# Decay attention and two MLPs on one core: a later arrival for the first weights in the planner, and one copy of the row maxima per unit

## The chip, the cores and the metric

The kernel runs on one core of a Trainium2 chip. The core has five engines with instruction streams of their own: PE multiplies matrices, DVE, ACT and POOL work on vectors, and SP mainly issues transfers (DMA). An engine takes its instructions in order: one that waits holds up all behind it on its engine. The metric is the device time of one execution in microseconds (us). Three runs of the kernel before gave a median of 1074.44 us (1074.03 to 1074.98).

## The reference

Three stages, all in float32:

- attention with decay, for 4 batches of 8 heads, 576 positions, 64 wide: the scores are `q k^T / 8` plus `cum[s] - cum[t]`, where `cum` is the running sum of `log(clip(f, 1e-4, 1))`; positions behind the diagonal are masked; a softmax, with the row's maximum subtracted before the exponential; the result times `v`
- a first MLP on the 2304 rows of 512: `h = x @ w_in` (512 x 2048), `h * sigmoid(1.702 h)`, times `w_out` (2048 x 512)
- a second MLP of the same shape, with `max(h, 0) + alpha * min(h, 0)` between its two products

## The kernel before

**How float32 is multiplied.** An operand is split into a high and a low part in the format fp32r, and a product is taken as high x high, high x low and low x high. Splitting costs a rounding copy (helpers L354 on ACT, L356 on DVE) and a subtraction (L359 on DVE or POOL). Weights come through a longer conversion. `weight` calls `convert` for the half of `w_in` and the half of `w_out` that belong to 128 of the 2048 hidden columns. `convert` loads 512 KB into one of three raw buffers (`p_raw8`, L475), runs L479 and L480 on ACT, L481, L484 and L487 on DVE (the last on POOL at times), and then the split (L354, L359).

**Units of attention.** A unit is one batch, one pair of heads and one part of the positions: 0 to 255 (the first half, 16 units) or 256 to 575 (the second half, 16 units). `prep` loads and splits q, k and v. `chunk` finds the row maxima: PE computes the scores of each 128-row tile and head (L602, or L595 and L596 for a last tile of 64 rows, which holds both heads), DVE adds the mask and takes the maximum of each row into one column of a tile `MX` (L611). A matmul of `MX` with an identity turns these columns into rows of a PSUM bank (L627), and copies with the factor -1 bring the rows into `DQ` (L636 on ACT or L638 on DVE), one copy per tile and head. A turning matmul holds up to four jobs, one per tile and head, each in its own 32 columns. A unit of the first half has one such matmul and four copies, one of the second half two matmuls and six copies. A column beside each maximum holds -1.0, which gives the ones that multiply `cum` in `DK`.

`chunk2` computes the scores again, transposed, as four products per head (L663). The last of them is `DK` times `DQ` and adds the decay and subtracts the maximum; so it needs the copies. ACT takes the exponentials (L667), POOL clears what is behind the diagonal (L671), PE multiplies with v (L683, L689, L712), and DVE divides (L722 to L742) into `xr`.

**The MLPs.** As soon as 256 positions are finished for all heads, `mlp1a` runs the first 8 of the 16 weight slices over them (L755 for the hidden layer, L797 for the output), between the units of attention. After attention the other 8 slices follow (L755, L878), then the second MLP (L755, L907).

**What sets the order.** Nothing in the order is written by hand. Every operation is given to a `Plan` with its engines, its cost in ns, what it reads and writes, and a priority. `Plan.run` then goes through them when the kernel is built: it takes, again and again, the operation that can start earliest by its own account (the priority decides between equals), on the engine where it ends earliest. The engines get their instructions in that order. A transfer counts as finished at

```
end = max(t + 1500.0, dma) + dur + 750.0
```

where `dur` is its bytes over 360 and `dma` the end of the transfer before it. Whoever reads the result may start `LAT` = 230 later, plus the operation's own `lag`, which is 0 everywhere in the kernel before. The first eight weight slices are added with priorities of about 100 to 109, all others with 2000 and more. At the start POOL fills the buffers that keep constants (L417), `MX` among them (two buffers).

Of the kernel before, what the change touches and what calls it, by code (L numbers as in the profile page):

```python
# [7 lines left out]
F32 = mybir.dt.float32  # L8
# [10 lines left out]
BS = 200  # L19
WS = 0  # L20
BD = 300
QUEUE = {"SP": "SP", "ACTQ": "ACT"}


# [157 lines left out]
def kernel(  # L182
# [18 lines left out]
    P = 128  # L201
# [42 lines left out]
    def sb(reg, nm, slots, shape, dt=F32, after=()):  # L244
        p = Pool(slots, after)

        def make(i):
            side, cl = closing[reg]
            return open_region(reg, side, cl).tile(shape, dt, name=f"{nm}{i}", tag=f"{nm}{i}")

        p.make = make
        return p
# [33 lines left out]
    p_vr = sb("att", "VR", 2, [P, NKT, 2, P])  # L286
    p_vh = sb("att", "VH", 2, [P, 3, 2, P], F32R)
    p_vl = sb("att", "VL", 2, [P, 3, 3, D], F32R)
    p_mx = sb("att", "MX", 2, [P, 132], F32R)
    p_e = sb("att", "e", 4, [P, 2, 320])  # L290
    p_eh = sb("att", "eh", 2, [P, 2, 320], F32R)
    p_el = sb("att", "el", 2, [P, 2, 320], F32R)
# [68 lines left out]
    def a_copy(n):  # L361
        return [("ACT", c_act(n)), ("DVE", c_dve(n, True), BC + WC * n, True)]
# [37 lines left out]
    plan.add([("POOL", 870.0)], set_mask, (), [b_mask], -88)  # L400
    plan.add([("POOL", 700.0)], set_mask2, (), [b_mask2], -40)
    plan.add(a_copy(P), lambda e: copy(e, ident_r, ident), [b_id], [b_idr], -60)
    fill = {}
    for nm, p, view, n, val in (
        ("dk", p_dk, lambda x: (x.bitcast(F32), x[0:3].bitcast(F32), x[64:67].bitcast(F32)), 3 * S, (0.0, 1.0, 1.0)),
        ("z", p_z, lambda x: x.bitcast(F32), P, 0.0),
        ("dq", p_dq, lambda x: x.bitcast(F32), S - SPLIT, 0.0),
        ("mx", p_mx, lambda x: x.bitcast(F32), 132, -1.0),
        ("vr", p_vr, lambda x: x.rearrange("p t h c -> p t (h c)")[:, :, D:3 * D], NKT * P, 1.0),
        ("vh", p_vh, lambda x: x.rearrange("p t h c -> p t (h c)")[:, :, D:3 * D].bitcast(F32), 3 * P, 1.0),  # L410
        ("vl", p_vl, lambda x: x[:, :, 1].bitcast(F32), 3 * D, 0.0),
    ):
        for i in range(p.n):
            b = fill[nm, i] = Buf()
            p.tiles[i] = p.make(i)
            plan.add([("POOL", 0.95 * n + 60.0)], lambda e, p=p, i=i, view=view, val=val: [
                E[e].memset(x, y) for x, y in (zip(view(p.tiles[i]), val) if isinstance(val, tuple) else ((view(p.tiles[i]), val),))  # L417
            ], (), [b], -90 if nm in ("dk", "dq", "mx") and i == 0 else -70 if i == 0 else -40)
# [51 lines left out]
    def convert(wb, half, src, pri, lpri=None):  # L470

        raw, w = Buf(p_raw8), Buf(p_wc)
        sl = slice(half * KT, (half + 1) * KT)
        n = KT * P
        plan.add(DMA(P * n * 8), lambda e: nc.sync.dma_start(raw.ap.rearrange("p c n t -> p c (n t)"), src), (), [raw], pri if lpri is None else lpri)  # L475
        low, high = lambda: raw.ap[:, :, :, 0], lambda: raw.ap[:, :, :, 1]
        wi = lambda: w.ap.bitcast(I32)

        plan.add([("ACT", c_act(n))], lambda e: nc.scalar.mul(w.ap, high().bitcast(F32), 2.0 ** -112), [raw], [w], pri)  # L479
        plan.add([("ACT", c_act(n))], lambda e: nc.scalar.mul(low(), low().bitcast(U32), 2.0 ** -29), (), [(raw, 0)], pri)  # L480
        plan.add([("DVE", c_dve(n, True), 0.0, True)], lambda e: nc.vector.tensor_scalar(wi(), wi(), 3, None, op0=ALU.logical_shift_left), (), [w], pri)  # L481
        plan.add(
            [("DVE", c_dve(n), 0.0, True)],
            lambda e: nc.vector.scalar_tensor_tensor(low(), high(), -2 ** 31, low(), op0=ALU.bitwise_and, op1=ALU.bitwise_or),  # L484
            (), [raw], pri,
        )
        plan.add(a_sub(n), lambda e: E[e].tensor_tensor(wi(), wi(), low(), op=ALU.add), [raw], [w], pri)  # L487
        plan.add(a_copy(n), lambda e: copy(e, wb.ap[:, 0, sl], w.ap), [w], [(wb, (half, 0))], pri)
        plan.add(a_sub(n), lambda e: sub(e, wb.ap[:, 1, sl], w.ap, wb.ap[:, 0, sl].bitcast(F32)), [w, (wb, (half, 0))], [(wb, (half, 1))], pri)
# [82 lines left out]
    def chunk(u, q0, q1, pri):  # L572
        kh, dk, qh, dq, z = u["kh"], u["dk"], u["qh"], u["dq"], u["z"]
        mx = Buf(p_mx)
        fmx = filled("mx", p_mx)
        n = q1 - q0
        tiles = [(t, t * P, min(P, S - t * P)) for t in range(q0 // P, (q1 + P - 1) // P)]
        nt = len(tiles)

        jobs = []  # L580
        for j, (t, a, w) in enumerate(tiles):
            jobs += [(j, t, a, w, (hh,)) for hh in range(2)] if w == P else [(j, t, a, w, (0, 1))]
        ji = 0
        for j, t, a, w in [(j, *x) for j, x in enumerate(tiles)]:
            ext = a + w
            cols = []
            step = ext if ext <= 512 else ext // 2
            for c0 in range(0, ext, step):
                c1 = c0 + step
                pms = [Buf(ps_m) for _ in range(2 if w == P else 1)]  # L590

                def mm(e, pms=pms, a=a, w=w, c0=c0, c1=c1):
                    if w < P:
                        o = pms[0].ap[:, :c1 - c0]
                        nc.tensor.matmul(o, z.ap, kh.ap[:, c0:c1], start=True, stop=False)  # L595
                        nc.tensor.matmul(o, ones[:, 1], dk.ap[:, c0:c1], start=False, stop=True)  # L596
                        return
                    for x, y in ((qh, kh), (None, dk)):
                        for hh in range(2):
                            r = slice(64 * hh, 64 * hh + 64)  # L600
                            l = ones[r, 0, :w] if x is None else x.ap[r, a - q0:a - q0 + w]
                            nc.tensor.matmul(pms[hh].ap[:, :c1 - c0], l, y.ap[r, c0:c1], start=x is not None, stop=x is None)  # L602

                plan.add([("PE", 2 * c_mm(c1 - c0, P))], mm, [qh if w == P else z, kh, (dk, 0), (dk, 1), b_one, *u["fdk"]], pms, pri)
                for i, pm in enumerate(pms):
                    col = 32 * (ji + i) + (2 if c0 == 0 else 3)
                    if w == P:
                        mk, m0 = mask, 3 * P - t * P + c0
                    else:
                        mk, m0 = (mask, 0) if c1 < ext else (mask2, 0)  # L610
                    plan.add([("DVE", c_dve(c1 - c0) + 90.0)], lambda e, pm=pm, c0=c0, c1=c1, mk=mk, m0=m0, col=col: nc.vector.tensor_tensor_reduce(  # L611
                        pm.ap[:, :c1 - c0], pm.ap[:, :c1 - c0], mk[:, m0:m0 + c1 - c0], 1.0, NEG,
                        ALU.add, ALU.max, accum_out=mx.ap[:, col:col + 1],
                    ), [b_mask if mk is mask else b_mask2, *fmx], [pm, (mx, col)], pri)
                    cols.append(col)
            if w < P:
                x, y = cols
                plan.add([("DVE", 70.0, 0.0, True)], lambda e, x=x, y=y: nc.vector.tensor_tensor(
                    mx.ap[:, x:x + 1], mx.ap[:, x:x + 1].bitcast(F32), mx.ap[:, y:y + 1].bitcast(F32), op=ALU.max
                ), [(mx, y)], [(mx, x)], pri)  # L620
            ji += 2 if w == P else 1

        pt = Buf(ps_m)
        for i0 in range(0, len(jobs), 4):
            jb = jobs[i0:i0 + 4]
            rows = 32 * len(jb) - 29
            plan.add([("PE", 110.0)], lambda e, i0=i0, rows=rows: nc.tensor.matmul(  # L627
                pt.ap[0:rows, 32 * i0:32 * i0 + P], mx.ap[:, 32 * i0:32 * i0 + rows], ident_r, start=True, stop=True
            ), [mx, b_idr], [(pt, i0)], pri)
            for i, (j, t, a, w, hhs) in enumerate(jb):  # L630
                for g, hh in enumerate(hhs):
                    def ev(e, i0=i0, i=i, a=a, w=w, hh=hh, g=g):
                        d = dq.ap[64 * hh:64 * hh + 3, a - q0:a - q0 + w]
                        s_ = pt.ap[32 * i:32 * i + 3, 32 * i0 + g * w:32 * i0 + g * w + w]
                        if e == "ACT":
                            nc.scalar.mul(d, s_, -1.0)  # L636
                        else:
                            nc.vector.tensor_scalar_mul(d, s_, -1.0)  # L638

                    plan.add([("ACT", 280.0), ("DVE", 240.0)], ev, [(pt, i0), *u["fdq"]], [(dq, ("x", i0 + i, hh))], pri)  # L640
        return dict(u=u, q0=q0, q1=q1, pri=pri)

    def chunk2(x):
# [324 lines left out]
```

## Time and profile before

| | |
|---|---|
| median of 3 runs | 1074.44 us |
| the profiled execution's own time | 1074.68 us |
| its span, first to last instruction | 1072.9 us |
| granted TensorE clock, mean | 0.978 of full speed |
| PE busy | 1034.7 us (96%) |
| DVE busy | 691.2 us (64%) |
| ACT busy | 446.9 us (42%) |
| POOL busy | 125.6 us (12%) |

The page divides the span into 40 slices of 26.8 us and gives the busy share of each in tenths (9 is 90% or more). PEclk is the clock that PE was granted, in tenths of full speed.

```profile
PE   5768999999999899999999999999999999999998
DVE  5888987888888877959963359833434433444333
ACT  4557545664645565847742237411211210211111
PEclk7888999999999999999999999999999999999999
DMA  5576563332242111645653245400200100010001
```

The first four slices, some 107 us, are those in which PE is not full. Attention goes on to about 410 us, the first MLP's second part to about 690 us, and the second MLP fills the rest.

### The profile page before, as it was taken

The page shows a single profiled execution, that of the slowest core. Times are in us where ns is not written, and L with a number is a line of the kernel's source. Part 1 is how long each engine was busy: PE and PEld are TensorE (multiplying, and loading weights), DVE is VectorE, ACT ScalarE, POOL GpSimd, SP SyncE. Part 2 cuts the span into 40 slices and gives each one's busy share as a digit, 9 for nine tenths or more (in the row PEclk, how much of TensorE's full clock was granted, in tenths as well). Part 3 has the DMA queues.
Part 4 walks back from the last instruction along what each step waited for, and adds up shares of the span by engine and source line. Part 5 has one row for each costly group of instructions (what it writes and reads, how often), then busy time and mean ns, then how long its engine had stood idle before and what let it go on. Part 6 is the DMA issues. An engine that isn't in the chain of part 4 may idle for free.

```text
span 1072.9 us, 17784 instructions
## 1 busy us (share of the span) xinstructions
PE 1034.7 (96%) x6531; PEld 887.3 (83%) x6531; DVE 691.2 (64%) x1565; ACT 446.9 (42%) x1042; POOL 125.6 (12%) x192
## 2 busy tenths in 40 slices
PE   5768999999999899999999999999999999999998
PEld 3657888889998789998878898888888888898886
DVE  5888987888888877959963359833434433444333
ACT  4557545664645565847742237411211210211111
POOL 6223221120111111002100101200000000000000
PEclk7888999999999999999999999999999999999999
DMA  5576563332242111645653245400200100010001
GB/s 112 125 167 178 126 153 78 67 78 60 52 94 41 52 24 47 211 156 163 222 165 98 69 128 158 137 1 1 69 0 1 57 13 1 20 41 20 1 1 39
DMA packets 170055, 86.54 MB, mean 81 GB/s; under 512 B 127440, under 2 KB 155280, under 8 KB 169968
## 3 DMA queue, kind: packets, MB, share of 16 engines
q1 hardware_dynamic: 160720, 84.30, 28.7%
q10 hardware_dynamic: 9248, 1.12, 0.7%
q8 instruction: 51, 0.84, 0.3%
q14 instruction: 36, 0.29, 0.1%
HBM read 66.34 MB, written 19.02 MB: 80 GB/s over the span
## 4 chain that ended last, share of the span: by engine, by line
PE 89%; DMA 3%; DVE 3%; ACT 2%; POOL 1%; issue 1%; SPq 0%; ACTq 0%; POOLq 0%; DVEq 0%
PE bk L755 36%; PE bk L907 18%; PE bk L797 10%; PE bk L878 8%; PE bk L663 5%; PE bk L712 4%; PE bk L683 2%; PE bk L602 2%; DMA wraw<-in_moe_w_out_dram 1%; DMA wraw<-in_moe_w_in_dram 1%; PE bk L689 1%; DMA rk<-in_k_dram 1%; PE bk L595 1%; PE bk L627 0%; POOL DK L417 0%
## 5 line engine op out<-in xcount | busy, mean ns | idle before, releaser
L354 ACT CAST qgh<-qgg 128x512 fp32r<-128x512 f32 (+1 forms) x118 | 68.3, 579 | 334.3 <-DVE qgg L769 297.2
L766 DVE TENSOR_SCALAR qgg<-bk,alpha_sb 128x512 f32<-128x512 f32 (+1 forms) x80 | 55.4, 694 | 164.9 <-PE bk L755 164.8
L755 PE MATMUL bk<-qx,wB 128*128 128x512 f32 (+1 forms) x720 | 155.9, 368 | 0.0
L755 PEld LDWEIGHTS bk<-qx,wB 128*128 128x128 f32 x720 | 126.0, 189 | 22.6
L755 PE MATMUL bk<-xh,wA 128*128 128x256 f32 x576 | 121.5, 293 | 0.0
L359 DVE TENSOR_TENSOR qgl<-qgg,qgh 128x512 fp32r<-128x512 f32 (+1 forms) x117 | 74.7, 640 | 68.4 <-ACT qgh L354 51.8
L755 PE MATMUL bk<-qx,wA 128*128 128x512 f32 (+1 forms) x480 | 103.6, 368 | 0.0
L755 PEld LDWEIGHTS bk<-xh,wA 128*128 128x128 f32 x576 | 96.1, 193 | 7.0 <-issue 4.0
L755 PEld LDWEIGHTS bk<-qx,wA 128*128 128x128 f32 x480 | 84.2, 188 | 15.3
L797 PE MATMUL bk<-gh,wA 128*128 128x256 f32 x576 | 84.0, 289 | 3.1 <-ACT gh L354 3.1
L755 PE MATMUL bk<-xl,wA 128*128 128x256 f32 x288 | 82.2, 286 | 1.3 <-DVE xl L359 1.3
L611 DVE CUSTOM_DVE_ANT_0 bk<-bk,mask 128x512 f32<-128x512 f32 (+3 forms) x160 | 75.2, 493 | 10.8 <-PE bk L602 9.0
L797 PEld LDWEIGHTS bk<-gh,wA 128*128 128x128 f32 x576 | 74.6, 193 | 6.8 <-ACT gh L354 3.8
L667 ACT ACTIVATE e<-bk 128x320 f32<-128x320 f32 (+3 forms) x224 | 65.9, 365 | 22.5 <-PE bk L663 21.7
L907 PE MATMUL bk<-wA,qgh 128*128 128x512 f32 x288 | 71.9, 389 | 0.0
L907 PEld LDWEIGHTS bk<-wA,qgh 128*128 128x128 f32 x288 | 53.8, 188 | 11.0
L671 POOL TENSOR_SCALAR_AFFINE_SELECT e<-e 128x256 f32<-128x256 f32 (+1 forms) x80 | 33.8, 436 | 206.7 <-ACT e L667 189.4
L755 PEld LDWEIGHTS bk<-xl,wA 128*128 128x128 f32 x288 | 55.9, 194 | 1.6 <-DVE xl L359 1.5
L878 PE MATMUL bk<-qgh,wB 128*128 128x512 f32 (+1 forms) x240 | 54.4, 369 | 1.7 <-ACT qgh L354 1.7
L907 PE MATMUL bk<-wB,qgh 128*128 128x512 f32 x216 | 53.9, 389 | 0.0
L755 PE MATMUL bk<-qx,wC 128*128 128x512 f32 (+1 forms) x240 | 52.9, 368 | 0.0
L769 DVE SCALAR_TENSOR_TENSOR qgg<-bk,qgg 128x512 f32<-128x512 f32 (+1 forms) x80 | 50.8, 636 | 2.3
(156 smaller groups left out, 2028.0 us busy)
## 6 DMA issues: line engine op xcount, KB each, us to landing
wraw<-in_moe_w_in_dram SPq DMA_DIRECT2D x32, 512.0 KB
wraw<-in_moe_w_out_dram SPq DMA_DIRECT2D x32, 512.0 KB
xscr<-xr SPq DMA_DIRECT2D x9, 512.0 KB
ypscr<-yp SPq DMA_DIRECT2D x18, 256.0 KB
rk<-in_k_dram SPq DMA_DIRECT2D x64, 72.0 KB
VR<-in_v_dram SPq DMA_DIRECT2D x32, 128.0 KB
qxb<-xscr SPq DMA_DIRECT2D x16, 256.0 KB
qyp<-ypscr SPq DMA_DIRECT2D x16, 256.0 KB
```

Of the source, the lines that this page charges most:

```text
L354: nc.scalar.copy(dst, src)
L359: E[e].tensor_tensor(dst, a, b, op=ALU.subtract)
L611: plan.add([("DVE", c_dve(c1 - c0) + 90.0)], lambda e, pm=pm, c0=c0, c1=c1, mk=mk, m0=m0, col=col: nc.vector.tensor_tensor_reduce(pm.ap[:, ...
L663: nc.tensor.matmul(pss[hh].ap[:w, :m], x.ap[r, a:a + w], y.ap[r, s0 - q0:n], start=i == 0, stop=i == 3)
L667: plan.add([("ACT", c_act(m, True))], lambda e, hh=hh, pss=pss, e32=e32, w=w, m=m: nc.scalar.activation(e32.ap[:w, hh, :m], pss[hh].ap[:w, ...
L712: nc.tensor.matmul(pb[hh].ap[:l.shape[1], s0 - q0:n], l, rhs.ap[:w, hh, :m], start=st, stop=sp, skip_group_check=True,)
L755: nc.tensor.matmul(ph.ap[:, :n], wb.ap[:, a, c, :], x(c), start=(c == 0 and i == 0), stop=(c == KT - 1 and i == 2))
L766: plan.add([("DVE", c_dve(n) + 56)], lambda e: nc.vector.tensor_scalar(g.ap[:, :n], ph.ap[:, :n], 0.0, alpha_sb[:, m:m + 1], op0=ALU.min, ...
L769: plan.add([("DVE", c_dve(n))], lambda e: nc.vector.scalar_tensor_tensor(g.ap[:, :n], ph.ap[:, :n], 0.0, g.ap[:, :n], op0=ALU.max, op1=ALU.add
L797: nc.tensor.matmul(py[d // 2].ap[:, d % 2 * BLK:(d % 2 + 1) * BLK], W1[m].ap[:, a, KT + d, :], g.ap, start=(m == 0 and i == 0 and a == 0 a ...
L878: nc.tensor.matmul(py[d].ap[:, :n], W1[m].ap[:, a, KT + d, :], g.ap[:, :n], start=(m == NA and i_ == 0 and a == 0), stop=(m == NM - 1 and ...
L907: nc.tensor.matmul(py[t].ap, g.ap[:, t * P:(t + 1) * P], wo[:, a, KT * P:], start=(m == 0 and i_ == 0 and a == 0), stop=(m == NM - 1 and i ...
```

## The change

Two things are changed.

1. A weight load with a priority below 1000, which are those of the first eight slices, gets a `lag` of `WLAG` = 2500: the planner lets the readers of its data start 2500 ns later than before. The instructions are the same; their order may be another.
2. The row maxima lie in another layout of `MX` (208 columns for 132): 68 columns per tile, the maximum of head 0 in column 2 and that of head 1 in column 66 of these. So a matmul of 67 columns of `MX` gives head 0's three rows at rows 0 to 2 and head 1's at rows 64 to 66, where `DQ` wants them. There is one such matmul per tile: two in the first half, three in the second, all of them one operation of the plan. One copy of 67 rows and the whole width (256 or 320) then takes the place of the four or six. Rows 3 to 63 hold what stands in the other columns; they meet zeros in `DK`. In the tile of 64 rows both heads stand above each other in the partitions, so a second identity (`ident2`, two copies of 64 columns at the start) adds the two halves, and the columns are filled with -0.5 and 0 to suit. Its maximum over two stretches is now two operations of 64 rows, one per head, instead of one of 128. Each of the two `MX` buffers is filled by four memsets instead of one.

```diff
+WLAG = 2500.0
...
-    p_mx = sb("att", "MX", 2, [P, 132], F32R)
+    p_mx = sb("att", "MX", 2, [P, 208], F32R)
+    ident2 = att.tile([P, 64], F32R, name="ident2")
...
+    b_id2 = Buf()
+    for i in range(2):
+        plan.add(a_copy(64), lambda e, r=slice(64 * i, 64 * i + 64): copy(e, ident2[r], ident[r, r]), [b_id], [(b_id2, i)], -39)
...
-        ("mx", p_mx, lambda x: x.bitcast(F32), 132, -1.0),
+        ("mx", p_mx, lambda x: (x.bitcast(F32), x[:, 136:204].bitcast(F32), x[64:P, 138:139].bitcast(F32), x[0:64, 202:203].bitcast(F32)), 280, (-1.0, -0.5, 0.0, 0.0)),
...
-        plan.add(DMA(P * n * 8), lambda e: nc.sync.dma_start(raw.ap.rearrange("p c n t -> p c (n t)"), src), (), [raw], pri if lpri is None else lpri)
+        plan.add(DMA(P * n * 8), lambda e: nc.sync.dma_start(raw.ap.rearrange("p c n t -> p c (n t)"), src), (), [raw], pri if lpri is None else lpri, WLAG if pri < 1000.0 else 0.0)
...
-                    col = 32 * (ji + i) + (2 if c0 == 0 else 3)
+                    col = 68 * j + 64 * i + 2 if w == P else 204 + (c0 > 0)
...
-                plan.add([("DVE", 70.0, 0.0, True)], lambda e, x=x, y=y: nc.vector.tensor_tensor(
-                    mx.ap[:, x:x + 1], mx.ap[:, x:x + 1].bitcast(F32), mx.ap[:, y:y + 1].bitcast(F32), op=ALU.max
-                ), [(mx, y)], [(mx, x)], pri)
+                for hh in range(2):
+                    r, o = slice(64 * hh, 64 * hh + 64), 138 + 64 * hh
+                    plan.add([("DVE", 70.0, 0.0, True)], lambda e, r=r, o=o, x=x, y=y: nc.vector.tensor_tensor(
+                        mx.ap[r, o:o + 1], mx.ap[r, x:x + 1].bitcast(F32), mx.ap[r, y:y + 1].bitcast(F32), op=ALU.max
+                    ), [(mx, x), (mx, y), *fmx], [(mx, o)], pri)
...
-        for i0 in range(0, len(jobs), 4):
-            jb = jobs[i0:i0 + 4]
-            rows = 32 * len(jb) - 29
-            plan.add([("PE", 110.0)], lambda e, i0=i0, rows=rows: nc.tensor.matmul(
-                pt.ap[0:rows, 32 * i0:32 * i0 + P], mx.ap[:, 32 * i0:32 * i0 + rows], ident_r, start=True, stop=True
-            ), [mx, b_idr], [(pt, i0)], pri)
...
-                    plan.add([("ACT", 280.0), ("DVE", 240.0)], ev, [(pt, i0), *u["fdq"]], [(dq, ("x", i0 + i, hh))], pri)
+        def turn(e):
+            for j, (t, a, w) in enumerate(tiles):
+                nc.tensor.matmul(
+                    pt.ap[0:67, P * j:P * j + w], mx.ap[:, 68 * j:68 * j + 67], ident_r if w == P else ident2,
+                    start=True, stop=True, skip_group_check=True,
+                )
+
+        plan.add([("PE", 75.0 * nt + 40.0)], turn, [mx, b_idr, b_id2], [pt], pri)
+
+        def ev(e):
+            d, s_ = dq.ap[0:67, :n], pt.ap[0:67, :n]
+            if e == "ACT":
+                nc.scalar.mul(d, s_, -1.0)
+            else:
+                nc.vector.tensor_scalar_mul(d, s_, -1.0)
+
+        plan.add([("ACT", c_act(n, True)), ("DVE", c_dve(n))], ev, [pt, *u["fdq"]], [dq], pri)
```

## Rows read from the trace of the kernel before

**Rows 1.** The page's part 4: shares of the chain that ended last, by engine

```profile
PE 89%; DMA 3%; DVE 3%; ACT 2%; POOL 1%; issue 1%; SPq 0%; ACTq 0%; POOLq 0%; DVEq 0%
```

**Rows 2.** Stretches: from:to, length, PE, PEld, DVE, ACT, POOL busy, clock, DMA share, GB/s

```profile
57.00:64.00 7.00, 1.42 (x16) 1.11 (x15) 2.36 (x4) 2.83 (x6) 1.29 (x1) 0.72 0.76 138
64.00:100.00 36.00, 31.36 (x235) 26.64 (x235) 34.21 (x96) 27.61 (x69) 11.37 (x16) 0.83 0.63 166
100.00:130.00 30.00, 29.91 (x267) 24.62 (x267) 26.63 (x90) 18.98 (x52) 7.06 (x10) 0.98 0.57 137
130.00:420.00 290.00, 286.34 (x2503) 254.26 (x2501) 236.44 (x633) 160.59 (x461) 47.65 (x81) 0.99 0.31 67
```

**Rows 3.** Timeline around 62 us: start, length, instruction [idle before, what ended it]

```profile
62.39 0.66 ACT L479 ACTIVATE wc<-wraw 128x512 f32<-128x512 f32 x1 [4.10 <-DMA wraw<-in_moe_w_in_dram]
...
63.91 0.61 DVE L638 TENSOR_SCALAR DQ<-bk 3x128 fp32r<-3x128 f32 x2 [4.46 <-ACT DQ L636]
...
64.25 0.97 PE L663 MATMUL bk<-DQ,DK 64*128 64x256 f32 x2 [5.84 <-DVE DQ L638]
```

**Rows 4.** Chain of waits in order of time: start, length, what was waited for

```profile
55.85 6.45 DMA wraw<-in_moe_w_in_dram
```

**Rows 5.** Stretch behind the gap, columns as in rows 2

```profile
64.00:70.00 6.00, 5.75 (x30) 5.00 (x32) 5.84 (x17) 2.91 (x9) 1.92 (x3) 0.50 0.36 90
```

**Rows 6.** Copies of maxima: 0 to 130 us (min/median/max ns), and DVE's in 64 to 100

```profile
L636 ACT ACTIVATE DQ<-bk x33: 249/267/272, 17.8 to 129.2; 3x128 fp32r<-3x128 f32 x33
...
L638 DVE TENSOR_SCALAR DQ<-bk x19: 253/285/297, 18.2 to 129.5; 3x128 fp32r<-3x128 f32 x19
...
64.00:100.00 36.00, 0.78 (x3) 0.83 0.63 166
```

**Rows 7.** Waits: us in total, times, longest; 0 to 130 us, the second 64 to 100

```profile
DVE DQ L638 <- ACT DQ L636: 8.1, 9, 4.5
...
DVE DQ L638 <- ACT DQ L636: 5.8, 2, 4.5
...
ACT wc L479 <- DMA wraw<-in_moe_w_out_dram: 4.9, 4, 2.6
ACT wc L479 <- DMA wraw<-in_moe_w_in_dram: 4.1, 1, 4.1
```

**Rows 8.** ACT reading a 128x256 bank, 0 to 130 us: busy us, mean ns

```profile
L761 ACT ACTIVATE gg<-bk 128x256 f32<-128x256 f32 x12 | 4.6, 383 | 4.5 <-PE bk L755 4.4
```

**Rows 9.** Timeline of one unit's copies at 30 us, columns as in rows 3

```profile
30.25 0.25 ACT L636 ACTIVATE DQ<-bk 3x128 fp32r<-3x128 f32 x1
...
31.52 0.29 DVE L638 TENSOR_SCALAR DQ<-bk 3x128 fp32r<-3x128 f32 x1
31.54 0.71 PE L663 MATMUL bk<-DQ,DK 64*128 64x256 f32 x2 [1.45 <-ACT DQ L636]
```

**Rows 10.** PE's timeline around two turning matmuls of the second half

```profile
167.57 0.28 PE L755 MATMUL bk<-xh,wA 128*128 128x256 f32 x1
167.69 0.28 PE L627 MATMUL bk<-ident_r,MX 128*99 128x128 f32 x2
167.81 0.33 PE L755 MATMUL bk<-xh,wA 128*128 128x256 f32 x1
```

**Rows 11.** Timeline of POOL at the start: the first fill of MX

```profile
0.81 0.21 POOL L417 MEMSET MX<- 128x132 f32 x1 [0.29 <-POOLq L952]
```

**Rows 12.** SP's issues of weight halves, the sixth and the sixteenth of the first eight slices

```profile
52.08 0.57 SPq L475 DMA_DIRECT2D wraw<-in_moe_w_out_dram  x1
...
98.76 0.36 SPq L475 DMA_DIRECT2D wraw<-in_moe_w_out_dram  x1
```

**Rows 13.** The first MLP on PE, 64 to 100 us: L755, then L797; PE, PEld busy

```profile
64.00:100.00 36.00, 10.02 (x54) 8.86 (x54) 0.83 0.63 166
64.00:100.00 36.00, 8.79 (x48) 7.64 (x48) 0.83 0.63 166
```

**Rows 14.** PE's timeline late in attention

```profile
369.36 0.22 PE L627 MATMUL bk<-ident_r,MX 128*3 128x128 f32 x1 [2.22 <-DVE MX L618]
```

More of the change, by code (lines that the diff above doesn't have):

```diff
@@ L578, in chunk @@
         nt = len(tiles)
[L580 to L583, printed above, removed]
         for j, t, a, w in [(j, *x) for j, x in enumerate(tiles)]:
@@ L617, in chunk @@
                 x, y = cols
-                plan.add([("DVE", 70.0, 0.0, True)], lambda e, x=x, y=y: nc.vector.tensor_tensor(
-                    mx.ap[:, x:x + 1], mx.ap[:, x:x + 1].bitcast(F32), mx.ap[:, y:y + 1].bitcast(F32), op=ALU.max
-                ), [(mx, y)], [(mx, x)], pri)
-            ji += 2 if w == P else 1
-        pt = Buf(ps_m)
-        for i0 in range(0, len(jobs), 4):
-            jb = jobs[i0:i0 + 4]
-            rows = 32 * len(jb) - 29
-            plan.add([("PE", 110.0)], lambda e, i0=i0, rows=rows: nc.tensor.matmul(
-                pt.ap[0:rows, 32 * i0:32 * i0 + P], mx.ap[:, 32 * i0:32 * i0 + rows], ident_r, start=True, stop=True
-            ), [mx, b_idr], [(pt, i0)], pri)
[L630 to L638, printed above, removed]
-                    plan.add([("ACT", 280.0), ("DVE", 240.0)], ev, [(pt, i0), *u["fdq"]], [(dq, ("x", i0 + i, hh))], pri)
```

## Prediction

> **What bounds the kernel now.** I read the page first: its chain of waits gives 89% of the span to PE [rows 1], so work taken from another engine counts only where PE is held up. The busy times by stretch say where that is. From 100 us on PE is busy 29.91 of 30 us and then 286.34 of 290 [rows 2]: that part is as long as PE's own work. Before it there are gaps, and the largest is 57 to 64 us, where PE works 1.42 of 7 us and DVE, ACT and POOL are idle for more than half of it. From 64 to 100 us DVE is busy 34.21 of 36 us, so there DVE sets the pace.
>
> The timeline of that gap names its cause [rows 3]. ACT reaches the first conversion of a weight half (L479) and sits 4.10 us until the bytes are there. The chain gives this transfer 6.45 us from its issue [rows 4]. Behind that instruction on the same engine stands a copy of the row maxima (L636), which needs nothing of the weight. The next copy, on DVE, waits 4.46 us for it and starts at 63.91; PE waits 5.84 us for both, with its scores all but the last product done. PE then starts again at a granted clock of 0.50, the 1.2 GHz level, and is busy 5.75 of 6 us there [rows 5].
>
> **The change part by part, against the profiled execution's own 1074.68 us** (span 1072.9 and 1.78 outside it; 0.24 above the median of 1074.44).
>
> *A, the lag.* The planner counts a weight half as there 1500 + 1456 + 750 + 230 ns = 3.94 us after its issue; this one took 6.45. With 2.5 us more it counts 6.44, so conversions of the first eight weights go behind work that is ready. If the copy of [rows 3] comes ahead of L479, it needs neither the bytes nor the wait. Ends: nothing comes back, or PE's 5.84 us and half of its 5.75 busy us at the slow level, 8.7 in all. Since DVE sets the pace behind the gap, I take what DVE can move into it, its 4.46 us of waiting: **-4.5**. Queued behind a later L479 are L480, DVE's four steps, the weight buffer's release and the next load on SP; nothing of attention waits for these. What is late next is the weights themselves (a rival, below).
>
> *B, one copy per unit.* A unit had four copies of 3x128 (six in the second half), 33 on ACT at 267 ns and 19 on DVE at 285 ns in the first 130 us [rows 6]. They follow each other from engine to engine: DVE waited 8.1 us for ACT's copies in 9 places, 5.8 of it in 64 to 100 us, of which 4.5 is A's wait [rows 7]. There is one copy of 67x256 now. The trace has no such copy; the nearest is ACT's read of a 128x256 bank, 383 ns [rows 8]; 267 ns is the lower end, four times that the upper. I take 383 ns, on ACT, which the planner's costs favour. Where DVE sets the pace, 64 to 100 us, it loses 0.78 us of copies and 1.3 us of waiting: -2.1. In the unit at 29 us the first copy begins at 30.25 and PE goes on at 31.54 after 1.45 us of waiting [rows 9]; one copy ends at 30.63, so 0.9 sooner. The other units' wait is hidden or held by transfers. **-3.0**; ends 0 and -7 (2.1, and a whole us in each of some five units before 57 us).
>
> The Trainium skill has a sentence against this (Perfetto Trace Analysis, Optimizing Scalar/DVE Operations): where ACT and DVE aren't saturated but hold up others, smaller instructions may let work end sooner. It would give a late copy: 383 instead of 267 ns, 0.12 us in each of 32 units, +3.7 at most. The rows differ from it: the small copies didn't run side by side; the last began 1.27 us after the first [rows 9].
>
> *C, more matmuls.* A unit's maxima were turned by one matmul (99 columns held, 128 streamed), or two; now by two or three of 67 held columns: 32 more. Two such issue within 0.12 us, 60 ns each [rows 10]. 32 x 60 ns = **+1.9**, all of it charged, since most fall where PE is full. Ends: 0 where PE idles, and 32 x 120 ns = 3.8 if holding 67 fresh columns is not hidden, by the 120 ns from the 256-column matmul ahead of them to the first.
>
> By the Trainium skill (TensorE: Matmul & The Clock Gate, Back-to-back issue gap) a load and a matmul of 128 columns sustain about 81 ns; the sum would then be +2.6 for this term, 0.7 more. Only the pair above bears on it.
>
> *D, the fills.* Each of the two buffers of maxima is filled by four memsets on POOL instead of one, which took 0.21 us for 132 columns [rows 11]: 208 columns, 68 columns, and twice a single one. Three more of at most that time are 0.6 us, and the columns alone are 0.2 us; I take 0.4 us a buffer. POOL's fills stand one behind the other at the start, and the fills of DK behind these two come ahead of SP's loads into DK. **+0.8**; ends 0 (ACT's logarithm and the transfers cover it) and 1.2. The two copies of the second identity lie at the start beside idle ACT.
>
> *E, the rest.* The second half has one more 134 ns maximum per unit on DVE, 16 x 134 = 2.1 us, and loses 3 to 5 small copies for it; PE is full there, except at 369.36, where it waited 2.22 us for the older maximum [rows 14]. I cost it at 0; ends -2.2 and +2.2, since the new order may drop that wait or make another. If PE ran dry there, each unit's 0.13 would show.
>
> Sum: -4.5 - 3.0 + 1.9 + 0.8 = -4.8: **1069.9 us**.
>
> **Rivals.** *The transfer is the bound (1074.4).* In 57 to 64 us the DMA share is 0.76 [rows 2]: bytes that land at 62.4 land there whatever ACT does, and the next units' k and q are behind them. Then A returns nothing and the rest is -3.0 + 2.7 = -0.3. For it: the chain's two transfers in a row. Against it: the last product, its exponentials, the sums over v and a slot of the first MLP stood ready. The same time comes out if the new order only puts another urgent instruction behind another late weight: ACT's waits on weights were 9.0 us in five places, this one 4.1 [rows 7].
>
> *Weights too late (slower, 1080.8).* Three raw buffers hold the weight halves. A hold that is 2.5 us longer by plan delays every third load by as much. From the sixth to the sixteenth half, 52.08 to 98.76 us, ten intervals are 4.67 us each [rows 12]; 10/3 x 2.5 makes the last 8.3 us later. In 64 to 100 us PE is busy 10.02 + 8.79 us with the first MLP, half of the stretch [rows 13]; without its weights that share idles: 8.3 x 0.52 = 4.3. A returns nothing, of B only 0.9 is left: 4.3 - 0.9 + 2.7 = +6.1. It decides where those ten intervals exceed about 5.5 us. For it: conversion is what PE lives on there. Against it: these loads now wait for stalled engines, not for the plan.
>
> *All of the gap and the clock (1063.5).* With the gap gone PE needn't start again at 0.50: -8.7 - 3.0 + 2.7, and the wait at 369 us goes too, -2.2: -11.2. Against it: DVE was busy 95% of the time behind the gap.
>
> **How the numbers follow.** Forecast 0.45, with a range of its own of 1066 to 1072; transfer-bound 0.20; weights too late 0.23; all of the gap 0.12. From 0.2% (2.1 us), about what a measurement of this kernel can tell, I call it faster or slower. The forecast and the large gain give faster 0.60, with a little from the second case; the second gives the same 0.17; the third slower 0.23. The range goes from just below the largest gain, 1062.5, to just short of the late weights, 1080, with 1 in 10 left out at either end.
>
> **What the next profile would show.** A right: no PE wait of over 2 us before 100 us that ends with a copy of maxima, and ACT's waits at L479 below 9.0 us in all. A wrong: the same gap between 55 and 70 us with another name, or DMA share over 0.9 in it. B right: 32 copies of some 0.38 us, no waits between ACT and DVE over them, DVE busier than 95% or the stretch shorter. C right: 80 turning matmuls 60 to 120 ns apart. D wrong: the first scores issue as early as before. The forecast falls if the sixteenth weight load is issued later than 98.76 us, or if PE idles more than 0.5 us in 100 to 130 us.

## The result, and the profile after

| | before | after |
|---|---|---|
| median | 1074.61 us (4 runs, 1074.03 to 1074.98) | 1064.47 us (4 runs, 1063.38 to 1066.33) |
| the profiled execution: time, span | 1074.68, 1072.9 us | 1064.79, 1063.1 us |
| granted clock, mean | 0.978 | 0.984 |

The ratio is 0.9906, with a 95% interval of 0.9883 to 0.9928: the changed kernel is faster by 10.1 us. The forecast was 1069.9 us, 4.8 us faster.

The page of the changed kernel gives the busy times of the engines; PE's work is 2.4 us shorter than before, the span 9.8 us:

```profile
PE 1032.3 (97%) x6563; PEld 886.8 (83%) x6563; DVE 680.9 (64%) x1523; ACT 433.3 (41%) x970; POOL 129.3 (12%) x202
```

So PE's idle time fell from 38.2 to 30.8 us (span less busy time). Of the 9.8 us, 7.4 are idle time of PE; the other 2.4 are busy time, and since 32 more turning matmuls stand in it (some 2 us), the rest of PE's work takes some 4 us less, at a mean clock of 0.984 for 0.978. The stretches say where. These are of the changed kernel, columns as in [rows 2]; four of them have the limits of [rows 2], and 64 to 70 us those of [rows 5]:

```profile
0.00:57.00 57.00, 40.95 (x306) 30.88 (x307) 43.84 (x143) 29.21 (x71) 24.54 (x63) 0.82 0.60 130
57.00:64.00 7.00, 3.89 (x35) 2.89 (x33) 4.90 (x16) 3.44 (x9) 2.45 (x4) 1.00 0.59 123
64.00:70.00 6.00, 4.95 (x32) 4.49 (x34) 4.62 (x15) 2.91 (x6) 1.99 (x2) 0.64 0.84 215
64.00:100.00 36.00, 31.76 (x235) 26.95 (x236) 30.83 (x90) 23.86 (x56) 7.64 (x11) 0.81 0.68 182
100.00:130.00 30.00, 28.64 (x266) 23.71 (x266) 26.64 (x90) 17.07 (x47) 10.57 (x15) 1.00 0.62 145
130.00:420.00 290.00, 289.14 (x2557) 259.56 (x2554) 236.73 (x615) 158.99 (x420) 55.52 (x88) 1.00 0.33 75
360.00:380.00 20.00, 20.00 (x176) 18.15 (x177) 15.25 (x41) 9.62 (x26) 2.52 (x5) 1.00 0.12 26
420.00:560.00 140.00, 139.81 (x799) 123.09 (x798) 109.22 (x200) 87.89 (x168) 10.06 (x7) 1.00 0.55 171
```

And four of the kernel before that are not among [rows 2]:

```profile
0.00:57.00 57.00, 39.38 (x277) 29.41 (x278) 40.83 (x144) 28.59 (x71) 25.67 (x59) 0.79 0.58 128
360.00:380.00 20.00, 17.26 (x137) 14.76 (x137) 17.70 (x48) 12.57 (x37) 3.77 (x7) 0.91 0.19 56
370.00:374.00 4.00, 3.83 (x28) 3.43 (x27) 3.70 (x10) 3.50 (x11) 0.00 (x0) 0.59 0.43 140
420.00:560.00 140.00, 138.27 (x823) 123.30 (x822) 117.27 (x221) 93.39 (x178) 13.33 (x10) 1.00 0.57 183
```

Length less PE's busy time is PE's idle time: up to 130 us 27.9 before and 24.8 after, from 130 to 420 us 3.7 and 0.9, from 420 to 560 us 1.7 and 0.2. From 130 to 420 us almost all that is gained lies between 360 and 380: there the traces hold 137 matmuls of PE before and 176 after, and the clock was 0.91 and is 1.00. That is the wait of [rows 14] and the 1.2 GHz level behind it (0.59 from 370 to 374 us). With 2.74 us idle and half of the some 3.6 us at the lower level (0.09 below full speed is a share of 0.18 at half of it), that place cost about 4.5 us in the profiled execution of before, by estimate, and costs nothing after.

The gap on which step A rests is not gone. The timeline of the changed kernel, columns as in [rows 3]:

```profile
60.39 0.66 ACT L485 ACTIVATE wc<-wraw 128x512 f32<-128x512 f32 x1 [2.57 <-DMA wraw<-in_moe_w_in_dram]
...
60.67 0.28 PE L759 MATMUL bk<-xh,wA 128*128 128x256 f32 x1
...
62.63 0.38 ACT L765 ACTIVATE gg<-bk 128x256 f32<-128x256 f32 x1
...
64.15 0.41 DVE L766 SCALAR_TENSOR_TENSOR gg<-gg,bk 128x256 f32<-128x256 f32 x1
...
64.59 0.41 ACT L356 CAST gh<-gg 128x256 fp32r<-128x256 f32 x1 [1.58 <-DVE gg L766]
...
65.05 1.57 PE L801 MATMUL bk<-gh,wA 128*128 128x256 f32 x8 [4.10 <-ACT gh L356]
```

L485 is the old L479. ACT stands at the same weight half as before, but only until 60.39 us: PE is still at its last product of the hidden layer then (L759, 60.67 us). Behind the half on ACT are three casts, a step of the conversion, the sigmoid of the first MLP (L765) and the cast gh, and no copy of maxima; DVE's product L766 comes between the last two. PE waits 4.10 us for this chain, where it waited 5.84 [rows 3]. So the weight pushes PE's next work back on ACT, but the wait for its bytes is over before PE's begins. ACT's waits at weights, up to 130 us, are 10.0 us and not 9.0 as in [rows 7]:

```profile
ACT wc L485 <- DMA wraw<-in_moe_w_in_dram: 6.2, 3, 2.6
ACT wc L485 <- DMA wraw<-in_moe_w_out_dram: 3.8, 3, 2.0
```

### The profile page after: what moved, and what is told of

Its sections match the earlier page's. It is cut to its first block, busy times and chain, and to the rows that moved or that the text cites. A ratio compares the mean times of both kernels' runs of the same rounds, so it can differ in the third digit from the quotient of the medians.

```text
span 1063.1 us, 17696 instructions
## 1 busy us (share of the span) xinstructions
PE 1032.3 (97%) x6563; PEld 886.8 (83%) x6563; DVE 680.9 (64%) x1523; ACT 433.3 (41%) x970; POOL 129.3 (12%) x202
## 4 chain that ended last, share of the span: by engine, by line
PE 89%; DMA 3%; DVE 3%; POOL 1%; ACT 1%; issue 1%; SPq 0%; ACTq 0%; DVEq 0%; POOLq 0%
PE bk L759 36%; PE bk L911 18%; PE bk L882 9%; PE bk L801 9%; PE bk L667 5%; PE bk L716 4%; PE bk L604 2%; DMA wraw<-in_moe_w_in_dram 2%; PE bk L687 2%; PE bk L693 1%; DMA wraw<-in_moe_w_out_dram 1%; PE bk L630 1%; DMA rq<-in_q_dram 1%; PE bk L597 1%; DVE wraw L490 0%
## 5 line engine op out<-in xcount | busy, mean ns | idle before, releaser
L759 PE MATMUL bk<-qx,wB 128*128 128x512 f32 (+1 forms) x720 | 155.5, 368 | 0.0
L759 PEld LDWEIGHTS bk<-qx,wB 128*128 128x128 f32 x720 | 126.0, 189 | 22.7
L759 PE MATMUL bk<-xh,wA 128*128 128x256 f32 x576 | 124.1, 295 | 0.0
L759 PE MATMUL bk<-qx,wA 128*128 128x512 f32 (+1 forms) x480 | 103.6, 368 | 0.0
L759 PEld LDWEIGHTS bk<-xh,wA 128*128 128x128 f32 x576 | 96.7, 194 | 7.3 <-issue 3.7
L759 PEld LDWEIGHTS bk<-qx,wA 128*128 128x128 f32 x480 | 84.2, 188 | 15.3
L759 PE MATMUL bk<-xl,wA 128*128 128x256 f32 x288 | 82.4, 286 | 0.0
L671 ACT ACTIVATE e<-bk 128x320 f32<-128x320 f32 (+3 forms) x224 | 64.9, 364 | 30.8 <-PE bk L667 26.6
L759 PEld LDWEIGHTS bk<-xl,wA 128*128 128x128 f32 x288 | 55.9, 194 | 0.0
L759 PE MATMUL bk<-qx,wC 128*128 128x512 f32 (+1 forms) x240 | 52.7, 368 | 0.0
L485 ACT ACTIVATE wc<-wraw 128x512 f32<-128x512 f32 x64 | 43.0, 676 | 23.0 <-DMA wraw<-in_moe_w_in_dram 14.5
```

Of the source, the lines that this page charges most:

```text
L671: plan.add([("ACT", c_act(m, True))], lambda e, hh=hh, pss=pss, e32=e32, w=w, m=m: nc.scalar.activation(e32.ap[:w, hh, :m], pss[hh].ap[:w, ...
L759: nc.tensor.matmul(ph.ap[:, :n], wb.ap[:, a, c, :], x(c), start=(c == 0 and i == 0), stop=(c == KT - 1 and i == 2))
```

## The experiments

Medians and ratios are against the kernel before on the same chip: 1074.07 us (1070.37 to 1078.32, 28 runs) for the first four, 1074.24 (1070.86 to 1076.88, 23 runs) for the next four, 1075.07 (1072.26 to 1078.91, 29 runs) for the last four. Single executions differ by some 0.4% either way here, so the medians judge, and a profile only says where time lies in one execution. The ratios and intervals are worked out from all executions and can differ from the quotient of the two medians by 0.07%.

| kernel | median us | ratio | 95% interval |
|---|---|---|---|
| lag alone | 1072.03 | 0.9988 | 0.9971 to 1.0005 |
| one copy, lag 0 | 1068.18 | 0.9952 | 0.9935 to 0.9970 |
| one copy, lag 1250 | 1074.76 | 1.0012 | 0.9996 to 1.0028 |
| one copy, lag 5000 | 1068.31 | 0.9954 | 0.9940 to 0.9969 |
| after, copies twice | 1064.38 | 0.9906 | 0.9887 to 0.9925 |
| after, turning matmuls twice | 1069.47 | 0.9951 | 0.9937 to 0.9965 |
| before's order, one copy, behind the weight | 1073.24 | 0.9993 | 0.9979 to 1.0006 |
| before's order, one copy, ahead of the weight | 1073.22 | 0.9989 | 0.9978 to 0.9999 |
| before's order, conversion later | 1075.72 | 1.0007 | 0.9994 to 1.0021 |
| after's order, conversion later | 1064.84 | 0.9905 | 0.9890 to 0.9921 |
| before's order, late maximum sooner | 1076.26 | 1.0007 | 0.9995 to 1.0018 |
| before, LAT 240 | 1073.33 | 0.9982 | 0.9968 to 0.9995 |

### The two parts, each alone, and the size of the lag

Lag alone:

```
-  plan.add(DMA(P * n * 8), ... [raw], pri if lpri is None else lpri)
+  plan.add(DMA(P * n * 8), ... [raw], pri if lpri is None else lpri, 2500.0 if pri < 1000.0 else 0.0)
```

> The kernel before with the 2500 ns lag and the old six or four copies. Theory (lag and copies add, sized as predicted): the lag takes away ACT's wait ahead of the copy at 62 us, -4.5 of 1074.6, so about 1070; no PE wait over 3 us that ends with a copy of maxima before 100 us. Rival 1 (the copies give it all, the lag only renames the gap): 1074 to 1075, with another PE gap of 4 us or more between 55 and 70 us. Rival 2 (any new order shifts the time by some us, with no part to thank): anything from 1065 to 1080, and e2 not fitting a sum.

The changed kernel with `WLAG = 0.0`:

> The changed kernel with WLAG = 0: the new copies and matmuls with the old arrival. Theory (as predicted: copies -3.0, matmuls +1.9, fills +0.8): about 1074.3, and together with e1 the two differences sum to the -10 of both. Rival 1 (the copies give it all): 1064 to 1066. Rival 2 (any new order shifts it): off both by over 2 us.

With `WLAG = 1250.0`:

> The changed kernel with half the lag, 1250 ns. If the lag works by its size, the time lies between e2 and the changed kernel's 1064.5. If it works only through where the list happens to put things, it lies outside of these two by over 1 us.

With `WLAG = 5000.0`:

> The changed kernel with twice the lag, 5000 ns. If late weights cost as the slower rival said (each third load later by the added hold), the sixteenth half is issued some 8 us later than 93.4 us and the time is 1067 to 1070. If the lag only has to cover the wait, 1063 to 1066. If only the order's chance decides, neither.

The lag alone gives 0.12%, with an interval that holds 1, the one copy alone 0.48%, both 0.94%. Neither came out as it was priced: 1072.03 us for 1070, and 1068.18 for 1074.3. With the one copy in place the time goes 0.9952, 1.0012, 0.9906, 0.9954 as the lag goes 0, 1250, 2500, 5000 ns (the third is the changed kernel's own ratio). The kernels of this row run the same instructions but for the choice of engine of some. Up to 2500 ns their weights aren't issued later either: the sixteenth half at 93.28, 93.84 and 93.39 us. So neither the issue of the weights nor the cost of a copy can be behind the 1.06% between 1250 and 2500 ns: it is the list that the planner writes. What that list has less of is idle time of PE: span less busy time is 35.3, 35.8, 30.8 and 36.3 us in the four profiles. Over these four values the lag has no direction.

With 5000 ns the sixteenth half is issued 8.5 us later than with 2500, as the first case of its expectation had it, and 1068.31 us lies in the 1067 to 1070 of that case. So at 5000 late weights may have a part in the time; this run doesn't separate them from the list. SP's issue with lag 5000:

```profile
101.91 0.38 SPq L481 DMA_DIRECT2D wraw<-in_moe_w_out_dram  x1
```

The stretch from 360 to 380 us shows that the late stall isn't the whole of it either. Lag alone, then lag 1250, columns as in [rows 2]; with lag 0 and 5000 PE is busy 20.00 us there too:

```profile
360.00:380.00 20.00, 20.00 (x182) 18.20 (x180) 14.46 (x38) 9.90 (x28) 3.66 (x6) 1.00 0.15 43
```

```profile
360.00:380.00 20.00, 19.58 (x173) 17.26 (x172) 14.38 (x40) 11.03 (x28) 3.18 (x5) 1.00 0.14 32
```

Nowhere here does PE stand as it did before, and yet these two kernels are within 0.2% of before. The trace of lag alone shows where it went there. The gap of [rows 3] is filled (PE busy 6.24 of 7 us), PE waits 3.64 us for a maximum instead, to 67.26 us, and from 100 to 130 us it idles 2.5 us and has a mean clock of 0.83, where before it idled 0.1 at 0.98 [rows 2]. In all its profile has 5.9 us less idle time than before (32.3) and 3.0 us more busy time (1037.6).

```profile
57.00:64.00 7.00, 6.24 (x60) 5.03 (x58) 6.13 (x17) 3.25 (x9) 2.12 (x3) 1.00 0.57 125
100.00:130.00 30.00, 27.54 (x215) 22.21 (x213) 24.27 (x79) 18.55 (x51) 6.78 (x11) 0.83 0.54 133
```

```profile
67.26 0.42 PE L627 MATMUL bk<-ident_r,MX 128*99 128x128 f32 x1 [3.64 <-DVE MX L611]
```

### What a copy and a turning matmul cost

In the changed kernel's order, each copy issued twice, and each turning matmul issued twice:

```
+  for _ in range(2):
       if e == "ACT":
           nc.scalar.mul(d, s_, -1.0)
...
```

> The changed kernel in its own order, with each of the 32 copies of 67 rows issued twice on the same engine; the planner is not told. Theory (the copies' own time and chain bring the gain): 32 more copies of 0.38 to 0.43 us give back 2 to 4 us, 1066.5 to 1068.5. Rival (the new order alone brings it): under 1 us, 1064.5 to 1065.5, since ACT is busy only 41%.

```
-  for j, (t, a, w) in enumerate(tiles):
+  for j, (t, a, w) in list(enumerate(tiles)) * 2:
...
```

> The changed kernel in its own order, with all 80 turning matmuls issued twice, the planner not told. If one costs the 60 ns of the pair in the trace of before and PE is full for most of them: +4.8 us, 1069.3. If holding 67 fresh columns is not hidden (120 ns): +9.6, 1074. If it falls into gaps: under 2 us.

32 more copies cost nothing that can be measured, within some 3 us to either side by the two intervals: 64 of them run in 1064.38 us. So the lower part of the 2 to 4 us of the first theory stays open here; the next section takes copies away instead. The trace of that kernel (instruction, count, min/median/max ns) shows that they are not short (52 on ACT here, the 12 on DVE have a median of 422 ns):

```profile
L641 ACT ACTIVATE DQ<-bk x52: 372/425/436, 17.4 to 395.4; 67x320 fp32r<-67x320 f32 x28, 67x256 fp32r<-67x256 f32 x24
```

80 more turning matmuls cost 5.0 us by the medians, 62 ns each; by the two ratios on that chip, 0.9951 and 0.9906, it is 4.8 us, with 2.5 us to either side. PE's timeline in that kernel shows them in pairs of the usual distance, three in 0.15 us:

```profile
159.34 0.29 PE L630 MATMUL bk<-ident_r,MX 128*67 128x128 f32 x2
159.46 0.19 PE L630 MATMUL bk<-ident,MX 128*67 128x64 f32 x1
159.49 0.32 PE L630 MATMUL bk<-ident_r,MX 128*67 128x128 f32 x2
```

### Steps A and B in the order of before

Both kernels keep one copy in every unit, the last but for the unit at the gap, and leave the other copies out (so most maxima are not subtracted), in the order of before; in the unit at the gap the first keeps the one behind the waiting conversion on ACT, the second the one on DVE that is ahead of it. So they differ in one instruction:

```
     if pri == A0 + 5:
-        return [x for x in o if x.eng == "ACT"][0]
+        return [x for x in o if x.eng == "DVE"][0]
     return o[-1]
```

> The kernel before in its own order, with one of the four or six copies of maxima left in each unit (the others are left out, so most maxima are not subtracted): the last one, but in the sixth unit the one on ACT that stands behind the weight wait at 62 us. So the gap stays and the copies' time goes. Theory (copies matter by themselves): -3 to -6 against before, 1068 to 1071. Rival (only the order matters): within 1 us of before, 1073 to 1075.

> As f3_one_copy_late, but the copy left in the sixth unit is the one on DVE that ran at 59.18 us, ahead of ACT's weight wait: one instruction of difference, so the PE gap of 5.84 us ahead of the last product goes. Theory (A as predicted): 4 to 6 us below f3. Rival (the transfer is the bound and the time is lost behind it): under 1.5 us below f3, with a new PE wait of 4 us or more before 75 us.

The gains are 0.07 and 0.11%, with intervals that end at 0.21 and 0.22%, and the two medians differ by 0.02 us, where A would have made it 4 to 6. In the first, PE waits for the copy; in the second the copy's product (L673, the old L663) runs at 59.87, and PE waits for the exponentials, which stand behind the same conversion (timeline, first the one, then the other):

```profile
63.87 0.58 PE L673 MATMUL bk<-DQ,DK 64*128 64x256 f32 x1 [5.26 <-ACT DQ L646]
```

```profile
59.87 0.39 PE L673 MATMUL bk<-DQ,DK 64*128 64x256 f32 x2 [1.04 <-DVE DQ L648]
...
62.70 0.66 ACT L479 ACTIVATE wc<-wraw 128x512 f32<-128x512 f32 x1 [3.67 <-DMA wraw<-in_moe_w_in_dram]
...
64.76 0.58 PE L765 MATMUL bk<-xh,wA 128*128 128x256 f32 x1 [3.83 <-ACT e L677]
```

That left room for step A in full, with all of that unit's work ahead of the conversion. The next kernel has it; the one behind it does the same in the changed kernel's order; a third takes away the late stall alone; the last is a control without any part of the change.

```
...
+  o1, o2, o3, o4, o5 = self.seven        # the conversion of the seventh half
+  o3.start = max(o3.start, o4.start - 0.25)
+  o1.start, o2.start = max(o1.start, o3.start - 0.6), max(o2.start, o3.start - 0.5)
   out.sort(key=lambda o: (o.start, o.seq))
```

> The order of before, and nothing new in it, but for the five instructions that convert the seventh weight half: the two on ACT go behind the copy of maxima, a cast, the exponentials and two more casts, and one on DVE goes to just ahead of its next one. PE's, POOL's and the DMA queues are as before. It is step A alone and complete: neither the copy nor the exponentials of that unit stand behind the weight any longer. Theory 1, step A as predicted: PE's 5.84 us wait before 64.25 us (rows 3) falls below 1.5 us, no other gap takes its place, 4.5 us less: ratio 0.996. Theory 2, the transfer sets this stretch: the wait at 64.25 goes and others of about its length come before 75 us, at the next instruction that needs the converted weights: ratio 0.999 to 1.001.

The wait at 64.25 is gone. The second theory had waits of about its length before 75 us; there are two, of 1.16 and 1.08 us. The stretch from 57 to 64 us, columns as in [rows 2], then 57 to 100 us, and PE's next waits over 1 us:

```profile
57.00:64.00 7.00, 6.50 (x49) 5.47 (x49) 6.24 (x21) 5.17 (x13) 3.33 (x4) 0.81 0.84 136
57.00:100.00 43.00, 35.15 (x268) 28.74 (x268) 36.48 (x107) 30.98 (x76) 13.59 (x18) 0.88 0.70 175
```

```profile
67.18 1.22 PE L804 MATMUL bk<-gh,wA 128*128 128x256 f32 x8 [1.16 <-ACT gh L358]
71.30 0.32 PE L670 MATMUL bk<-QH,KH 64*128 64x128 f32 x1 [1.08 <-ACT e L674]
79.17 1.22 PE L804 MATMUL bk<-gh,wA 128*128 128x256 f32 x8 [1.99 <-ACT gh L358]
94.08 0.32 PE L670 MATMUL bk<-QH,KH 64*128 64x128 f32 x1 [2.31 <-ACT e L674]
```

For the first of them, the cast gh stands behind the next weight half on ACT:

```profile
66.18 0.66 ACT L484 ACTIVATE wc<-wraw 128x512 f32<-128x512 f32 x1 [1.30 <-DMA wraw<-in_moe_w_out_dram]
66.74 0.39 ACT L358 CAST gh<-gg 128x256 fp32r<-128x256 f32 x1
```

Behind the one at 64.25, the kernel before has two such waits up to 100 us:

```profile
80.76 2.08 PE L797 MATMUL bk<-gh,wA 128*128 128x256 f32 x8 [1.94 <-ACT gh L354]
...
96.22 0.32 PE L663 MATMUL bk<-QH,KH 64*128 64x128 f32 x1 [1.47 <-ACT e L667]
```

PE worked 6.50 us from 57 to 64 us and not 1.42 [rows 2], 5.1 us more. Up to 100 us it is 2.4 us more (35.15 against 32.78, the sum of 1.42 and 31.36): PE's idle time from 64 to 100 us rose from 4.6 to 7.4 us, with two waits that are new, at 67.18 and 71.30, and one that is longer, 2.31 for 1.47. Of the 2.4 us the median shows nothing: 1.0007, and the interval allows 0.6 us of gain at most, where A had 4.5. This profile is of the fastest of its 12 executions, so the 2.4 us are not to be read as a gain that was kept.

```
...
+  o1.start, o2.start = i.start + 0.05, i.start + 0.1     # i: the cast gh on ACT
+  o3.start, o4.start = i.start + 0.15, i.start + 0.2
+  o5.start = max(o5.start, o4.start + 0.05)
```

> The changed kernel's order with the same move: the conversion of the seventh half on ACT behind the casts, the tanh and the cast gh on which PE waits 4.10 us before 65.05 us, on DVE behind the product L766. Theory 1, the wait is ACT's place in the queue alone: gh is cast near 62.3 us and not at 64.6, 2.6 us off, 1061.9 us beside 1064.5. Theory 2, the next weight (the wait for it ended at 67.02 us in the trace of the changed kernel) takes it back: the same as the changed kernel, ratio to before 0.990 to 0.991.

0.9905 beside 0.9906: nothing. The cast gh came at 63.64 us, not near 62.3; PE's wait of 4.10 us fell to 1.66, two others, of 0.98 and 1.00 us, came within the next 4 us, and ACT stood longer at the next weight half, 3.90 us for 2.02 (PE, then ACT):

```profile
64.09 1.22 PE L808 MATMUL bk<-gh,wA 128*128 128x256 f32 x8 [1.66 <-ACT gh L361]
```

```profile
69.08 0.67 ACT L490 ACTIVATE wc<-wraw 128x512 f32<-128x512 f32 x1 [3.90 <-DMA wraw<-in_moe_w_out_dram]
```

```
...
+  if o.tag == "soon":                     # L611 and L618 of the unit at 369 us
+      o.start = max(x.start for x in o.deps) + 0.25
```

> The order of before with one move on DVE: the last maximum (L611) and its join (L618) of the unit at 369 us go ahead of two transposes, a reciprocal and a sum, to right behind the PE product that they read. Everything else as before. Theory 1, the late stall is a part of what the new order gained: PE's 2.22 us wait before 369.36 us (rows 14) falls below 0.7 us, and the 4 us at the lower clock level behind it, which the trace shows from 370 to 374.6 us, go too: 1.5 to 3.5 us off, ratio 0.997 to 0.9985. Theory 2, something behind it takes it back: ratio above 0.9995, with a new PE wait over 1 us before 420 us.

The wait for the maximum fell to 0.75 us, and 3 us later PE waited 2.29 us for DVE's division of the sums (L750), which stood behind it now:

```profile
369.89 0.22 PE L635 MATMUL bk<-ident_r,MX 128*3 128x128 f32 x1 [0.75 <-DVE MX L624]
...
373.08 0.63 PE L671 MATMUL bk<-QH,KH 64*128 64x320 f32 x1 [2.29 <-DVE xr L750]
```

`LAT = 240` in place of 230:

> A control: the kernel before, with no part of the change, but with the planner's constant for the hand-over between engines at 240 and not 230, so that it writes another list of the same work. Theory 1, the gain of the changed kernel comes from its parts (the lag and the one copy): this one stays within 0.2% of before. Theory 2, lists of this planner scatter by as much as the change moved: it goes off by 0.3% or more to either side, 1064 to 1080 us, with PE's idle time before 130 us (27.9 us) or from 130 to 560 us (5.4 us) changed by over 3 us.

0.18% faster: inside the 0.2% of the first theory, with an interval that ends at 0.32%. PE's idle time before 130 us is as before (27.7 us), and from 130 to 560 us it is 2.3 for 5.4 us, without the late stall. So three lists with the old copies (before, lag alone, `LAT` 240) lie within 0.18% of each other, and the four with one copy within 1.06%, 0.9956 in the mean: the wide scatter is shown for lists with one copy alone. Whether lists with one copy are also faster on the whole, these seven don't settle.

## Why the prediction was right or wrong

**The time** was forecast on the right side and half as large as it was: inside the stated range (1062.5 to 1080), outside the forecast's own (1066 to 1072). That it fell inside is luck in good part. Two of the terms, A and B, hold in no experiment, and what came in their place is a term that the prediction had at 0.

**A (-4.5) failed**, at the step "I take what DVE can move into it". What the prediction named as the sign against A is there: the same gap between 55 and 70 us with another name, and ACT's waits at weights at 10.0 us and not below 9.0. The lag alone fills the gap and gains 0.29% at most, 3.1 us; the kernel that does all of A at this gap and nothing else gains 0.6 us at most. Behind the late weight ACT had several things that PE was to want (a copy, exponentials, casts), and with all of them ahead of the weight PE ran dry again a little later: half of what was gained in the gap was given back by 100 us, at the cast gh, which then stood behind the eighth half, and at the next exponentials. That is the rival "the transfer is the bound", in the form that the new order only puts another urgent instruction behind another late weight. Whether it is the bytes or the conversion's own chain that sets this stretch, these runs don't separate: the DMA share is 0.84 in the emptied gap, and the conversion of the seventh half begins at 62.39 us in the one and at 62.53 in the other.

**B (-3.0) failed** as a price of the copies. With the order held and all but one copy of each unit gone, the gain is 0.07%, and the interval's end is 0.21%, 2.3 us. In the changed order the copies may be doubled at no cost that shows (some 3 us to either side). The row behind it was read rightly (DVE's waits for ACT's copies are gone, and DVE is busy 30.83 of 36 us from 64 to 100 us, 86% where it was 95% [rows 2]), but the stretch didn't get shorter for it: PE is busy 31.76 us there, 31.36 before. DVE's 95% was not the bound.

The copies themselves came out near what was taken, 423 and 421 ns for 383, with 6 of the 32 on DVE (changed kernel, columns as above):

```profile
L640 ACT ACTIVATE DQ<-bk x26: 379/423/434, 17.4 to 394.3; 67x320 fp32r<-67x320 f32 x14, 67x256 fp32r<-67x256 f32 x12
L642 DVE TENSOR_SCALAR DQ<-bk x6: 382/421/488, 54.3 to 288.8; 67x256 fp32r<-67x256 f32 x4, 67x320 fp32r<-67x320 f32 x2
```

The sentence of the Trainium skill (Perfetto Trace Analysis, Optimizing Scalar/DVE Operations) that smaller instructions may let work end sooner finds no support here and nothing against it: neither more nor fewer copies moved the time by what these runs can tell.

**C (+1.9) was right**: 62 ns each where 60 were taken. The Trainium skill's 81 ns for a load and a matmul of 128 columns (TensorE: Matmul & The Clock Gate, Back-to-back issue gap) would make 6.5 us for the 80, an estimate; the trace has three in 0.15 us, and the interval of the measurement, 29 to 92 ns, holds both.

**D (+0.8)** took 0.4 us a buffer; it is 0.58. POOL's next fill begins 0.72 us behind the start of the first fill of `MX` (0.81 us in both kernels), and 0.14 before (the changed kernel, then before):

```profile
1.53 0.36 POOL L423 MEMSET DQ<- 128x320 f32 x1
```

```profile
0.95 0.37 POOL L417 MEMSET DQ<- 128x320 f32 x1
```

That this reaches the end isn't shown. The first score issues 1.5 us later (11.62 for 10.12 us), but the last product of that unit's scores 0.54 us sooner (12.44 for 12.98), the first weight load 0.55 us later (15.34 for 14.79), and PE's idle time up to 57 us is 16.0 us, 17.6 before.

**E (0) was the mis-sized term.** It is the one that prices the new order, with ends of -2.2 and +2.2; neighbouring values of the lag differ by 1.06%, 11 us. Its lower end was the wait of [rows 14] alone; in the profiled pair that place was worth some 4.5 us, since behind the wait PE ran at the 1.2 GHz level for most of 370 to 374 us. It went because the new list puts other work there. It is not had by mending the wait itself: with the maximum moved up, DVE, which in that kernel works almost without a break from 365.7 to 373.5 us, is late with the division of the sums instead. Nor is it enough: lag alone, lag 1250 and `LAT` 240 are without the stall and gain 0.18% at most.

**What the 10 us are then.** Shown: the lists of this planner differ by as much as 1.06% when nothing but the lag's value changes, and in two kernels with the changed order (copies doubled, conversion moved) the gain stays at 0.94 and 0.95%. In the profiled pair it lies at 0 to 130 us (3.2 us less idle time), at 369 us (some 4.5 us) and at 420 to 560 us (1.5 us). Not shown: which moves of the list before 130 us do it. Three lists without the late stall are no faster than before, or by 0.18%, and single waits that were taken out before 130 us returned nothing, so the gain is no sum of single waits that one could have read from the profile of before. That the lag models the transfers better, or that the one copy saves its own time, is not what makes this kernel faster, as far as these runs can tell: the copies left out in the old order return 2.3 us at most. That the one copy lets the planner write better lists on the whole is not excluded.

**The rivals.** "All of the gap and the clock" (1063.5) came out nearest in time, and not by its mechanism: the gap is still 4.10 us, and PE starts behind it at 0.64 from 64 to 70 us (0.50 in [rows 5]). "Weights too late" is out: the sixteenth half is issued at 93.39 us, 5.4 us sooner than in [rows 12]; only with twice the lag does it come late. One sign that the forecast had named for its own fall did come, PE idle for 1.36 us between 100 and 130 us, and cost little beside the rest.

```profile
93.39 0.35 SPq L481 DMA_DIRECT2D wraw<-in_moe_w_out_dram  x1
```

## What to carry to other kernels

When a planner writes the order, an edit to its costs or its work can be above all a draw of another list: price what the edit adds and removes, but give the new order a term with both signs, as wide as neighbouring values of the constant make it, and measure several values before believing in one. A wait that a trace shows is worth its length only if nothing else that PE needs stands behind the same late transfer or the next one; take it out alone in the old order, and see what PE waits for next.

## What the runs showed that was not expected

- The kernel before ran in 1074.03 to 1074.98 us in four runs, and in 1070.37 to 1078.91 us on the chips of the experiments. With a scatter of 0.4% either way, a profile of one execution can lie 4.0 us from its kernel's median (lag 5000, 1072.28 for 1068.31).
- Holding 67 fresh columns for a matmul of 128 or 64 was hidden: 62 ns by the medians, three matmuls in 0.15 us by the trace.
- The granted clock of one stretch is no measure of the gain: the kernel with one copy ahead of the weight has 0.95 from 64 to 100 us, where the one before has 0.83 [rows 2] and the changed one 0.81, and it is as slow as before.
